# One accumulator in two weight slots, and a new order of decode and eviction in the steps of two chained MLP layers

## The chip, the cores and the metric

The kernel runs on one core of a Trainium2 chip. The metric is device time in microseconds (us) of one execution. Lower is better. Three runs of the kernel before are given, and one execution of it was profiled.

## The reference

A block-wise linear attention with decay gives a token matrix x of 1536 x 512. Two MLP layers follow, each with weights of its own:

```python
h = x @ w_in                                   # 1536x512 @ 512x2048
g = h * np.tanh(log1p(exp(h)))                 # layer 1 (mish)
x = g @ w_out                                  # 1536x2048 @ 2048x512
h = x @ w_in2
g = h * (1.0 / (1.0 + np.exp(-h)))             # layer 2 (silu)
out = g @ w_out2
```

All of it is in 32 bit. The change lies in the two layers; the attention is not touched.

## The kernel before, in words

**Tiling.** The 1536 tokens are three tiles of 512 (t = 0, 1, 2). The hidden size of 2048 is 16 blocks of 128 per layer. Blocks are taken two at a time, so a layer has 8 pairs and the two layers have pairs p = 0 to 15. Pairs 0 to 3 run beside and just behind the attention. From p = 4 on, each pair is one object `Step(p)`, written out by hand as a plan. `NF // 2` is 8, so step 8 is the first of layer 2, step 9 has no plan of its own before and runs the one called `steady`, and step 15 is the last.

**Precision.** Each 32-bit operand is held as a high part `hi` (rounded on ScalarE, `copy`, L237 and others) and a low part `lo` (what is left, a subtraction on GpSimd, L238, or on VectorE). A product is three passes: hi x hi, lo x hi, hi x lo.

**Fewer products.** For token tiles 0 and 1 together a step uses a seven-product scheme on 2 x 2 blocks, for both matrix products: `m1 m5 m6 m2 m7 m3 m4` (input side, L1080 to L1111) and `s1 s5 s6 s2 s7 s3 s4` (output side, L1262 to L1303), six matmuls each. It needs sums of blocks of x (`sums[0]` to `sums[3]`, made once per layer) and sums of blocks of the weights (`sum_pair`, called T for the input side and S for the output side). Step 8 has no T and uses eight plain products instead, `e0` to `e3`. Token tile 2 is computed plainly: `h0`, `h1` (12 matmuls each) and `o0`, `o1` (12 each). A usual step therefore has 42 + 24 + 24 + 42 matmuls of 128 x 512.

**PSUM.** Eight banks `Z[0]` to `Z[7]` are shared by all of it by hand. `quad[0]` is Z0 and Z1, `quad[2]` is Z4 and Z5, `quad[3]` is Z6 and Z7. `o0` and `o1` sum into four banks `po`, which `o1` then adds to the accumulator of tile 2 (L1241; copied on ScalarE, L1239, in step 8). `s1` then copies quad 3 to quad 0 on ScalarE (L1265), and `s6` goes on summing there. `into` (L1273) adds a quad to an accumulator on VectorE (L1279), or in step 8, where the accumulator is new, copies it on ScalarE (L1277).

**Weights.** A block of weights arrives packed, 512 KB, in one of four `slots` (L58, L111). `run_pre` (in plans `p`, `p4`, `p5`) issues two ScalarE activations that begin the decoding (L137, L138); `p4` and `p5` put the intermediate into the free bank Z4 or Z5, and plain `p` leaves it in SBUF. `run_split` (`d`) issues the next small operation of a list: a block takes two VectorE operations (L169, L173), the second of which gives the slot back; the sums of a pair take four on GpSimd (L206). `run_parts` (`w`) takes the next finished weight tile and makes its hi (L237) and lo (L238). After each visit of a plan (between semicolons) `pump` issues the loads for which a slot is free.

**Order.** Each engine runs its instructions in the order in which the plans issue them. A later instruction never passes one that waits.

**Between the layers.** The results of layer 1 stand in three accumulators, `accs[0, t]`. `a0` and `a1` are those of tiles 0 and 1. From them come the block sums of layer 2, partly in place: `s_1` makes the first two, `s_3` writes a0 - a1 into the first half of `a1` (L1338), `s_4` changes the second half of `a0` (L1341), and `s_5` makes the hi parts of sums 3 and 2 on ScalarE; `low3` and `low2` make their lo parts on VectorE (L1309). Tile 0's accumulator of layer 2, `accs[1, 0]`, takes the place of `a0`, and `accs[1, 1]` that of `a1`, so they are first written (L1277) when all that read the old ones has ended. The sums are used in step 9: sum 0 in `m5`, 1 in `m6`, 2 in `m7`, 3 in `m3`.

Of the kernel before, what the change touches and what calls it, by code (L numbers as in the profile page):

```python
# [7 lines left out]
F32 = mybir.dt.float32  # L8
# [9 lines left out]
def decay_attention_mish_silu_kernel(  # L18
# [8 lines left out]
    nc = tc.nc  # L27
    P = 128
# [7 lines left out]
    T = 512  # L36
# [3 lines left out]
    NF = w1.shape[0]  # L40
# [7 lines left out]
    const = ctx.enter_context(tc.tile_pool(name="const", bufs=1))  # L48
    xp = ctx.enter_context(tc.tile_pool(name="xp", bufs=NB))
    accp = ctx.enter_context(tc.tile_pool(name="accp", bufs=1))  # L50
# [4 lines left out]
    ps_o = banks.enter_context(tc.tile_pool(name="ps_o", bufs=2, space=PSUM))  # L55

    ctx.enter_context(tc.manual_schedule())
    slots = [const.tile([P, 1024], F32, name=f"slot{i}") for i in range(4)]  # L58
    arena = const.tile([P, 32, T], F32R, name="arena")
    places = [(arena, k) for k in range(32)]  # L60
    free = list(range(32))
# [5 lines left out]
    def take(weight=False):  # L67
        taken[0] += weight
        k = free.pop(0)
        whole_tile, j = places[k]  # L70
        t = whole_tile[:, j]
        lent[id(t)] = (k, t)
        return t
# [13 lines left out]
    def room():  # L87
        return len(free) > 1 and taken[0] + 2 <= quota[0]
# [13 lines left out]
    held = {}  # L102
# [23 lines left out]
    def split_w(n, i, pair=False):  # L126


        def begin(place=None):
            if place is not None:  # L130
                made[n, i] = place
            decs[n, i] = wdec.tile([P, 512], U32, tag="dec", name="dec")
            uses[n, i] = 1 + pair
            begun[n, i] = tick[0]
            low, high = raws[n, i][:, :, 0], raws[n, i][:, :, 1]
            d = made[n, i] if (n, i) in made else decs[n, i].bitcast(F32)
            nc.scalar.activation(d, high.bitcast(F32), AF.Copy, scale=2.0**-112)  # L137
            nc.scalar.activation(low, low, AF.Copy, scale=TOP3, bias=2.0**-21 - 0.5)  # L138

        def op(k):  # L140
            split_op(k, raws[n, i], decs[n, i], made.get((n, i)))
            if k == 1:
                slots.append(held.pop((n, i)))
                parts.append((decs[n, i].bitcast(F32), (n, i)))

        pre.append(((n, i), begin))
        todo.extend(((n, i), lambda k=k: op(k)) for k in range(2))
# [4 lines left out]
    def run_pre(k=1, age=1, place=None):  # L152
        while k and pre and len(uses) < WD and pre[0][0] in raws and tick[0] - loaded[pre[0][0]] >= age:
            pre.pop(0)[1](place)
            k -= 1

    def used(key):
        if key in uses:
            uses[key] -= 1
            if not uses[key]:  # L160
                del uses[key]

    def split_op(k, raw, d, place):


        low, high = raw[:, :, 0], raw[:, :, 1]
        e = d if place is None else place.bitcast(U32)
        if k == 0:
            nc.vector.scalar_tensor_tensor(  # L169
                out=e, in0=e, scalar=3, in1=low, op0=ALU.logical_shift_left, op1=ALU.bitwise_or  # L170
            )
        else:
            nc.vector.scalar_tensor_tensor(  # L173
                out=d, in0=high, scalar=0x80000000, in1=e, op0=ALU.bitwise_and, op1=ALU.bitwise_or
            )
# [43 lines left out]
    def run_parts(k=None):  # L219
        for _ in range(len(parts) if k is None else min(k, len(parts))):  # L220
            if not room():
                break
            f, key = parts.pop(0)
            homes_of[key] = take(True), take(True)
            hi, lo = [t.rearrange("p (k c) -> p k c", k=2) if len(key) > 2 else t for t in homes_of[key]]
            wtiles[key] = hi, lo
            if len(key) > 2:
                uses_left[key] = 1
            elif key[0] < GF:
                uses_left[key] = (3, 6)[key[1]]  # L230
            elif key[0] < 2 * GF:
                uses_left[key] = (2, 3)[key[1]]
            else:
                uses_left[key] = 2
            ready.add(key)
            used(key)
            nc.scalar.copy(hi, f)  # L237
            nc.gpsimd.tensor_tensor(out=lo, in0=f, in1=hi.bitcast(F32), op=ALU.subtract)  # L238

    def run_split(k, age=1):  # L240
        while k and todo and (todo[0][0] is None or (todo[0][0] == "sum" and not scratch) or begun.get(todo[0][0], 1 << 30) <= tick[0] - age):
            todo.pop(0)[1]()
            k -= 1
# [25 lines left out]
    def warm(n):  # L269
# [12 lines left out]
        out=unit, in_=unit, pattern=[[1, C]], base=1 - C, channel_multiplier=1, compare_op=ALU.not_equal, fill=1.0  # L282
# [260 lines left out]
    accs = {}  # L543
# [117 lines left out]
    def cast(i, f):  # L661
        return lambda: nc.scalar.copy(sums[i][0], f)

    def low(i, f):
        hi, lo = sums[i]
        return lambda: nc.vector.tensor_tensor(out=lo, in0=f, in1=hi.bitcast(F32), op=ALU.subtract)

    def tt(out, in0, in1, op):
        return lambda: nc.vector.tensor_tensor(out=out, in0=in0, in1=in1, op=op)
# [11 lines left out]
    sums = []  # L681
# [136 lines left out]
    for hh in range(2):  # L818
        for p in range(NP):
            h = H - 1 - (2 * p + hh)  # L820
            nc.vector.tensor_tensor_scan(
                out=whole_mask[:, hh, p], data0=lams[:, h : h + 1].to_broadcast([P, C]), data1=unit, initial=0.0,
# [54 lines left out]
    for i, (t, f) in enumerate(steps):  # L877
        n = i + PH
        if n == N:
# [11 lines left out]
                out=eye, in_=eye, pattern=[[1, P]], base=0, channel_multiplier=-1, compare_op=ALU.not_equal, fill=1.0  # L891
# [12 lines left out]
        lows = len(later)  # L904
# [97 lines left out]
    for item in items:  # L1002
# [7 lines left out]
        lows = len(later)  # L1010
# [26 lines left out]
    add, sub = ALU.add, ALU.subtract  # L1037
    tt = nc.vector.tensor_tensor
# [4 lines left out]
    class Step:  # L1043
# [186 lines left out]
        def o1(self):  # L1230
            self.o(1, self.po)
            if self.opens:
                accs[1, 2] = homes[-1].tile([P, 4, T], F32, tag="acc", name="acc")
            if self.seeded:
                return
            acc = accs[self.mm, 2]
            for k in (2, 0, 1, 3):
                if self.opens:
                    nc.scalar.copy(acc[:, k], self.po[k])  # L1239
                else:  # L1240
                    tt(out=acc[:, k], in0=self.po[k], in1=acc[:, k], op=add)  # L1241
# [25 lines left out]
        def s5(self):  # L1267
            self.second(2, 0, 0, True)
            if self.opens:
                accs[1, 0] = accp.tile([P, 4, T], F32, tag="acc", name="acc")  # L1270
            self.into(0, 2, 2, True)

        def into(self, t, a, src, fresh=False):  # L1273
            for k in range(2):
                to = accs[self.mm, t][:, a + k]
                if fresh and self.opens:
                    nc.scalar.copy(to, self.quad[src][k])  # L1277
                else:
                    tt(out=to, in0=self.quad[src][k], in1=to, op=add)  # L1279

# [24 lines left out]
    a0, a1 = accs[0, 0], accs[0, 1]  # L1305
# [8 lines left out]
    lows = {}  # L1314
# [12 lines left out]
    def c(t, k, e):  # L1327
        cast_x(t, k)(e)
# [6 lines left out]
        lows[1] = cast(sums[1], g[1])  # L1335

    def s_3():
        tt(out=a1[:, 0:2], in0=a0[:, 0:2], in1=a1[:, 0:2], op=sub)  # L1338

    def s_4():  # L1340
        tt(out=a0[:, 2:4], in0=a0[:, 2:4], in1=F[:, 0:2], op=sub)  # L1341

    def s_5():
        lows[3] = cast(sums[3], a0[:, 2:4])
        lows[2] = cast(sums[2], a1[:, 0:2])

    def turn(st):
        for i in range(8):
# [9 lines left out]
    def close(st):  # L1358
# [9 lines left out]
        for k, c in PIECES:  # L1368
            tt(out=acc[:, k, c], in0=st.po[k][:, c], in1=acc[:, k, c], op=add)
            nc.sync.dma_start(out_tiles(2)[:, k, c], acc[:, k, c])  # L1370

    extras = {"x2": x2, "s_1": s_1, "s_3": s_3, "s_4": s_4, "s_5": s_5}
    extras |= {f"low{i}": lambda i=i: low(i) for i in range(4)}
    extras |= {f"c{t}{k}": lambda t=t, k=k: c(t, k, nc.gpsimd if k > t else nc.vector) for t in range(2) for k in range(2)}
    extras |= {"p": lambda: run_pre(1, 0), **{f"p{i}": lambda i=i: run_pre(1, 0, st.Z[i]) for i in (4, 5)}, "d": lambda: run_split(1, 0), "w": lambda: run_parts(1)}
    tail = "m7 d d; m3; m4 ts; h0 a0 q0 n4 w; l0 p4 h1 a1 q1 w; l1 p5 o0 d d d d; o1 w w d d; s1 d d; s5 w; s6; s2 w; s7; s3; s4 p4"
    steady = "m1 p5 d d d d; m5; m6 w w; m2 d d; " + tail
    plans = {
        GF: "m1 p4 p5; m5; m6 d d d d; m2 w w d d; " + tail,
        NF // 2 - 1: "m1 p5 d d d d; m5; m6 w w; m2; m7; m3 ts; m4 n4 q0; h0 a0 l0; h1 a1 l1 q1; "  # L1380
        "s1; s5 table w; s6 p w; s2; s7 c01 seed; s3 c00; s4 c11 c10; o0 s_1; o1",
        NF // 2: "e0 low0 low1 x2 d d; e1 s_4 p w; e2 s_3 d d; e3; h0 a0 w l0 d d d d ts; h1 a1 s_5 l1 n4 q0 w q1 w low3; p o0; o1; s1 p; s5 d d w d d w; s6 low2 d d d d; s2; s7 w w; s3; s4 p4",
        NF - 1: "m1 p5 d d d d; m5; m6 w w d d d d; m2; m7 w w; m3 ts; m4 n4 q0; h0 a0 l0; h1 a1 l1 q1; s1; s5; s6; s2; s7; s3; s4; o0; o1",
    }
    adder[0] = nc.gpsimd
# [5 lines left out]
    for p in range(GF, NF):  # L1391
        st = Step(p)
# [55 lines left out]
```

## Time and profile before

| what | value |
|---|---|
| median of 3 runs | 556.21 us (556.08 to 556.86) |
| profiled execution, its own time | 556.43 us |
| its span, first to last instruction | 554.3 us |
| TensorE (PE) busy | 542.9 us, 98% |
| VectorE (DVE) busy | 401.9 us, 72% |
| ScalarE (ACT) busy | 340.8 us, 61% |
| GpSimd (POOL) busy | 287.8 us, 52% |
| granted TensorE clock | 0.998 |

A busy share is time in which an engine had an instruction running. PE is TensorE's matmul, PEld its weight load, which runs ahead of the matmuls. SPq is the queue that issues the loads of weights. In a timeline, the bracket at the end of a row is the engine's idle time just ahead of the row and the instruction that ended it.

### The profile page before, as it was taken

Reading aid. Unit: us, or ns where it says so; the run is one execution under the profiler, and the core shown is the slowest. Engines: PE = TensorE matmul, PEld = TensorE weight load, DVE = VectorE, ACT = ScalarE, POOL = GpSimd, SP = SyncE. Lnnn points to the kernel's source line nnn. Section 1 sums busy time; section 2 is a strip of 40 time slices with the busy share of each in tenths; the row PEclk is TensorE's granted clock in tenths of the full one; section 3 lists DMA queues with packets and bytes.
Section 4 is the critical chain, followed back from the end, with each engine's and each line's share of the span. In section 5 each row is a group of like instructions: output and inputs, shape, how many; then the busy total and the mean of one; then the engine's idle time right before and its main releaser. Section 6 shows DMA issues by size and latency. Waiting matters only on the chain.

```text
span 554.3 us, 8859 instructions
## 1 busy us (share of the span) xinstructions
PE 542.9 (98%) x3306; PEld 437.5 (79%) x3306; DVE 401.9 (72%) x639; ACT 340.8 (61%) x622; POOL 287.8 (52%) x269
## 2 busy tenths in 40 slices
PE   9999999999999999999999989999999999999995
PEld 6888778888877788888878767888887888888875
DVE  4887956994575695877867976686768595867684
ACT  4778553862654847566665877666575747565631
POOL 3555620322033775939220574957666675849610
PEclk9999999999999999999999999999999999999999
DMA  8993450231112222222200222222212122220006
GB/s 297 406 315 125 141 167 1 79 113 38 39 43 70 77 76 78 76 77 76 77 0 2 76 76 77 76 77 74 78 40 78 37 77 76 77 76 1 1 0 228
DMA packets 14602, 49.85 MB, mean 90 GB/s; under 512 B 1632, under 2 KB 1888, under 8 KB 14560
## 3 DMA queue, kind: packets, MB, share of 16 engines
q1 hardware_dynamic: 14560, 49.29, 26.3%
q8 instruction: 26, 0.43, 0.3%
q14 instruction: 16, 0.13, 0.1%
HBM read 46.14 MB, written 3.15 MB: 89 GB/s over the span
## 4 chain that ended last, share of the span: by engine, by line
PE 82%; DVE 9%; ACT 5%; issue 2%; POOL 1%; DMA 0%; SPq 0%; DVEq 0%; POOLq 0%; ACTq 0%
PE z L1255 19%; PE z L1066 16%; PE z L1157 10%; PE z L1212 9%; PE ph L588 7%; PE po L616 6%; PE pu L637 5%; PE b L733 1%; PE s L353 1%; PE px L406 1%; DVE xl L1309 1%; PE a L733 1%; PE warm L273 1%; DVE dec L173 1%; PE px L396 1%
## 5 line engine op out<-in xcount | busy, mean ns | idle before, releaser
L238 POOL TENSOR_TENSOR arena<-dec,arena 128x512 fp32r<-128x512 f32 x49 | 64.3, 1319 | 118.9 <-ACT arena L237 113.2
L1255 PE MATMUL z<-arena 128*128 128x512 f32 x376 | 97.7, 394 | 2.1 <-ACT acc L1277 1.2
L1279 DVE TENSOR_TENSOR acc<-z,acc 128x512 f32<-128x512 f32 x136 | 84.6, 683 | 10.8 <-PE z L1255 10.8
L1255 PEld LDWEIGHTS z<-arena 128*128 128x128 f32 x376 | 69.6, 188 | 20.2 <-ACT z L1265 3.1
L1149 POOL TENSOR_TENSOR arena<-F,arena 128x1024 fp32r<-128x1024 f32 x20 | 48.2, 2412 | 49.3 <-ACT arena L1148 49.3
L1157 PE MATMUL z<-xh,arena 128*128 128x512 f32 x168 | 53.8, 389 | 0.0
L238 POOL TENSOR_TENSOR arena<-t,arena 128x512 fp32r<-128x512 f32 x34 | 45.8, 1354 | 15.4 <-ACT arena L237 15.4
L237 ACT CAST arena<-dec 128x512 fp32r<-128x512 f32 x56 | 34.7, 620 | 29.7 <-DVE dec L173 29.6
L1212 PE MATMUL z<-arena 128*128 128x512 f32 x188 | 52.4, 390 | 0.3 <-DVE F L1139 0.3
L1066 PE MATMUL z<-xh,arena 128*128 128x512 f32 x182 | 50.0, 390 | 0.3 <-DVE z L1098 0.2
L138 ACT ACTIVATE slot<-slot 128x512 uint32<-128x512 uint32 x64 | 42.7, 668 | 0.0
L1212 PEld LDWEIGHTS z<-arena 128*128 128x128 f32 x188 | 35.2, 188 | 8.1 <-DVE F L1139 0.8
L237 ACT CAST arena<-t 128x512 fp32r<-128x512 f32 x38 | 23.5, 619 | 28.7 <-POOL t L206 23.0
L1066 PEld LDWEIGHTS z<-xh,arena 128*128 128x128 f32 x182 | 34.0, 188 | 8.3 <-DVE z L1098 0.7
L588 PE MATMUL ph<-xh,arena 128*128 128x512 f32 x124 | 39.2, 393 | 0.0
L137 ACT ACTIVATE z<-slot 128x512 f32<-128x512 f32 x40 | 25.4, 636 | 19.0 <-DVE acc L1279 19.0
L1157 PEld LDWEIGHTS z<-xh,arena 128*128 128x128 f32 x168 | 31.5, 188 | 6.5
L169 DVE SCALAR_TENSOR_TENSOR z<-z,slot 128x512 uint32<-128x512 uint32 x40 | 27.8, 695 | 10.3 <-ACT slot L138 10.0
L1157 PE MATMUL z<-xl,arena 128*128 128x512 f32 x88 | 34.2, 389 | 0.0
L637 PE MATMUL pu<-arena 128*128 128x512 f32 x132 | 33.8, 400 | 0.2 <-ACT arena L237 0.2
L206 POOL TENSOR_TENSOR t<-dec 128x256 f32<-128x256 f32 x42 | 31.3, 745 | 0.0
L616 PE MATMUL po<-arena 128*128 128x512 f32 x128 | 30.7, 393 | 0.1
(250 smaller groups left out, 1228.3 us busy)
## 6 DMA issues: line engine op xcount, KB each, us to landing
slot<-w SPq DMA_DIRECT2D x64, 512.0 KB, 4.2
xslot<-x SPq DMA_DIRECT2D x24, 512.0 KB, 7.5
out<-F SPq DMA_DIRECT2D x8, 256.0 KB, 2.1
out<-acc SPq DMA_DIRECT2D x3, 256.0 KB, 2.7
out<-acc SPq DMA_DIRECT2D x2, 128.0 KB, 2.5
factors<-lam SPq DMA_DIRECT2D x1, 0.0 KB
```

The lines of the kernel that those rows point to most:

```text
L138: nc.scalar.activation(low, low, AF.Copy, scale=TOP3, bias=2.0**-21 - 0.5)
L237: nc.scalar.copy(hi, f)
L238: nc.gpsimd.tensor_tensor(out=lo, in0=f, in1=hi.bitcast(F32), op=ALU.subtract)
L588: nc.tensor.matmul(ph, lhsT=wi[wsel][:, kk * P : (kk + 1) * P], rhs=xt[xsel][:, kk, :], start=(i == 0), stop=(i == 3 * KD - 1),)
L616: nc.tensor.matmul(po[t][j][:, c], lhsT=lhsT, rhs=rhs, start=(first and wsel + gsel == 0), stop=(last and gsel == 1 and c.stop == T),)
L637: nc.tensor.matmul(banks[j], lhsT=wtiles[f, 1][ws][:, js[j] * P : js[j] * P + P], rhs=gts[f, t][gs], start=(i < 2), stop=(i >= len(passes) ...
L1066: nc.tensor.matmul(self.Z[dst], lhsT=w[ws][:, kk * P : (kk + 1) * P], rhs=x[xx][:, kk, :], start=(start and i == 0), stop=True, skip_group ...
L1149: low.tensor_tensor(out=lo, in0=f, in1=hi.bitcast(F32), op=sub)
L1157: nc.tensor.matmul(z, lhsT=w[ws][:, kk * P : (kk + 1) * P], rhs=x[xx][:, kk, :], start=(i == 0), stop=True, skip_group_check=True,)
L1212: nc.tensor.matmul(banks[k], lhsT=lhsT, rhs=rhs, start=(j == 0 and ws + gs == 0 and not self.seeded), stop=True, skip_group_check=True,)
L1255: nc.tensor.matmul(self.quad[dst][k], lhsT=w[ws][:, k * P : (k + 1) * P], rhs=g[gs], start=(start and i == 0), stop=True, skip_group_check ...
L1279: tt(out=to, in0=self.quad[src][k], in1=to, op=add)
```

## The change

- `accs[1, 0]` gets storage of its own: slots 2 and 3 become the two halves of one tile, `slab`. When the two output-side weight blocks of step 8 are decoded, their slots go to a list `kept` that is never used again, and `s5` of step 8 takes `slab` as the accumulator. From then on there are two slots instead of four.
- `s_3` writes a0 - a1 into the first half of `a0`. `s_5` is split into `hi2` and `hi3`, which move from `h1` to `s7` of step 8; `low2` moves from `s6` to `s3`, and `low3` from `h1` of step 8 to `m6` of step 9, behind that visit's VectorE addition.
- In step 8 the decoding of the next blocks starts earlier (`p` in `h1` instead of with `o0`), and the two copies of `s4` go to VectorE (`into` with t = 1 and a = 2).
- `steady`: two of the four `d` of `m1` move behind `m6`'s product and addition.
- `tail` (steps 4 to 6 and 9 to 14): the two decodes start as `p6` (bank Z6) behind `l0` and `p4` behind `q1`, instead of `p4` behind `l0` and `p5` behind `l1`; the first `d` stands ahead of `l1`.
- `o1` adds its banks in the order 0, 1, 2, 3 instead of 2, 0, 1, 3, other than in step 8.

```diff
@@ slots
-    slots = [const.tile([P, 1024], F32, name=f"slot{i}") for i in range(4)]
+    slab = const.tile([P, 2048], F32, name="slab")
+    slots = [const.tile([P, 1024], F32, name=f"slot{i}") for i in range(2)]
+    slots += [slab[:, 1024 * i : 1024 * i + 1024] for i in range(2)]
+    kept = []
@@ split_w, op
-                slots.append(held.pop((n, i)))
+                (kept if n // 2 == NF // 2 and i else slots).append(held.pop((n, i)))
@@ o1
-            for k in (2, 0, 1, 3):
+            for k in (2, 0, 1, 3) if self.opens else range(4):
@@ s5, into
-                accs[1, 0] = accp.tile([P, 4, T], F32, tag="acc", name="acc")
+                accs[1, 0] = slab.rearrange("p (a c) -> p a c", a=4)
...
-                    nc.scalar.copy(to, self.quad[src][k])
+                    (nc.vector.tensor_copy if t and a else nc.scalar.copy)(to, self.quad[src][k])
@@ block sums of layer 2
-        tt(out=a1[:, 0:2], in0=a0[:, 0:2], in1=a1[:, 0:2], op=sub)
+        tt(out=a0[:, 0:2], in0=a0[:, 0:2], in1=a1[:, 0:2], op=sub)
...
-    def s_5():
-        lows[3] = cast(sums[3], a0[:, 2:4])
-        lows[2] = cast(sums[2], a1[:, 0:2])
+    def hi(i):
+        lows[i] = cast(sums[i], a0[:, 2 * i - 4 : 2 * i - 2])
@@ plans
-for i in (4, 5)}
+for i in (4, 5, 6, 7)}
-    tail = "m7 d d; m3; m4 ts; h0 a0 q0 n4 w; l0 p4 h1 a1 q1 w; l1 p5 o0 d d d d; o1 w w d d; s1 d d; s5 w; s6; s2 w; s7; s3; s4 p4"
-    steady = "m1 p5 d d d d; m5; m6 w w; m2 d d; " + tail
+    tail = "m7 d d; m3; m4 ts; h0 a0 q0 n4 w; l0 p6 h1 a1 q1 p4 w; d l1 d o0 d d; o1 w w d d; s1 d d; s5 w; s6; s2 w; s7; s3; s4 p4"
+    steady = "m1 p5 d d; m5; m6 d d w w; m2 d d; " + tail
-        NF // 2: "e0 low0 low1 x2 d d; e1 s_4 p w; e2 s_3 d d; e3; h0 a0 w l0 d d d d ts; h1 a1 s_5 l1 n4 q0 w q1 w low3; p o0; o1; s1 p; s5 d d w d d w; s6 low2 d d d d; s2; s7 w w; s3; s4 p4",
+        NF // 2: "e0 low0 low1 x2 d d; e1 s_4 p w; e2 s_3 d d; e3; h0 a0 w l0 d d d d ts; h1 a1 p l1 n4 q0 w q1 w d d; o0; o1 ; s1 p w; s5 d d; s6 d d d d w; s2; s7 hi2 w hi3 w; s3 low2; s4 p4",
+        NF // 2 + 1: steady.replace("m6", "m6 low3"),
```

## Rows read from the trace of the kernel before

**Rows 1.** The page, busy time of each engine, share of the span, instructions.

```profile
PE 542.9 (98%) x3306; PEld 437.5 (79%) x3306; DVE 401.9 (72%) x639; ACT 340.8 (61%) x622; POOL 287.8 (52%) x269
```

**Rows 2.** The chain that ended last, step 11: start, length, what.

```profile
393.24 9.69 PE z L1066 x42
...
408.37 5.44 PE z L1212 x24
413.81 9.67 PE z L1255 x42
```

**Rows 3.** Windows, step 8 and step 9's input side: length, busy time of engines.

```profile
295.59:330.53 34.94, 32.53 (x139) 25.60 (x138) 32.41 (x37) 27.60 (x48) 15.33 (x13) 1.00 0.19 61
330.53:342.30 11.77, 10.41 (x43) 7.65 (x42) 5.34 (x9) 8.79 (x17) 8.77 (x10) 1.00 0.28 90
```

**Rows 4.** Timeline of step 8, ScalarE, VectorE and TensorE: start, length, engine, line.

```profile
313.50 1.03 ACT L1308 CAST xh<-acc 128x1024 fp32r<-128x1024 f32 x1
...
316.04 0.68 DVE L1191 TENSOR_TENSOR F<-z,F 128x512 f32<-128x512 f32 x1
...
317.99 0.39 PE L1255 MATMUL z<-arena 128*128 128x512 f32 x1
...
318.32 0.66 ACT L137 ACTIVATE dec<-slot 128x512 f32<-128x512 f32 x1
...
319.44 2.03 ACT L1239 COPY acc<-z 128x512 f32<-128x512 f32 x4
...
320.06 1.67 PE L1255 MATMUL z<-arena 128*128 128x512 f32 x6 [0.54 <-ACT acc L1239]
...
322.01 3.03 PE L1255 MATMUL z<-arena 128*128 128x512 f32 x12 [0.28 <-ACT z L1265]
...
323.47 1.07 ACT L1277 COPY acc<-z 128x512 f32<-128x512 f32 x2
...
325.65 2.04 ACT L1277 COPY acc<-z 128x512 f32<-128x512 f32 x4
...
326.28 4.42 PE L1255 MATMUL z<-arena 128*128 128x512 f32 x18 [1.24 <-ACT acc L1277]
```

**Rows 5.** Timeline of step 9's input side, TensorE.

```profile
334.82 0.73 PE L1066 MATMUL z<-sh,more 128*128 128x512 f32 x2 [0.78 <-ACT z L1082]
...
338.08 1.19 PE L1066 MATMUL z<-sh,arena 128*128 128x512 f32 x4 [0.25 <-DVE z L1090]
```

**Rows 6.** Timeline of step 8, VectorE and GpSimd, both working on SBUF.

```profile
316.64 3.56 DVE L1149 TENSOR_TENSOR arena<-F,arena 128x1024 fp32r<-128x1024 f32 x2
...
317.03 4.33 POOL L238 TENSOR_TENSOR arena<-t,arena 128x512 fp32r<-128x512 f32 x2 [0.15 <-ACT arena L237]
...
320.12 2.31 DVE L1309 TENSOR_TENSOR xl<-acc,xh 128x1024 fp32r<-128x1024 f32 x1
```

**Rows 7.** Timeline of step 11, all engines, a steady step.

```profile
397.80 0.69 DVE L1090 TENSOR_TENSOR z<-z,F 128x512 f32<-128x512 f32 x1
...
398.55 0.30 PEld L1066 LDWEIGHTS z<-sh,more 128*128 128x128 f32 x2 [0.29 <-DVE z L1090]
...
400.25 0.70 DVE L1098 TENSOR_TENSOR z<-z,F 128x512 f32<-128x512 f32 x1 [1.75 <-PE z L1066]
...
411.21 0.61 ACT L237 CAST arena<-t 128x512 fp32r<-128x512 f32 x1
...
411.73 0.63 ACT L137 ACTIVATE z<-slot 128x512 f32<-128x512 f32 x1
...
414.39 2.48 DVE L1241 TENSOR_TENSOR acc<-z,acc 128x512 f32<-128x512 f32 x4
...
415.77 1.17 ACT L1265 COPY z<-z 128x512 f32<-128x512 f32 x2 [0.63 <-DVE acc L1241]
416.39 1.23 PEld L1255 LDWEIGHTS z<-arena 128*128 128x128 f32 x6 [0.28 <-ACT z L1265]
```

**Rows 8.** Instructions of the weight loads, L111, from 262 to 425 us.

```profile
DMA to landing us min/median/max: 3.5/4.2/4.7
```

More of the change, by code (lines that the diff above doesn't have):

```diff
@@ L1370, in close @@
             nc.sync.dma_start(out_tiles(2)[:, k, c], acc[:, k, c])
-    extras = {"x2": x2, "s_1": s_1, "s_3": s_3, "s_4": s_4, "s_5": s_5}
+    extras = {"x2": x2, "s_1": s_1, "s_3": s_3, "s_4": s_4, "hi2": lambda: hi(2), "hi3": lambda: hi(3)}
     extras |= {f"low{i}": lambda i=i: low(i) for i in range(4)}
     extras |= {f"c{t}{k}": lambda t=t, k=k: c(t, k, nc.gpsimd if k > t else nc.vector) for t in range(2) for k in range(2)}
-    extras |= {"p": lambda: run_pre(1, 0), **{f"p{i}": lambda i=i: run_pre(1, 0, st.Z[i]) for i in (4, 5)}, "d": lambda: run_split(1, 0), "w": lambda: run_parts(1)}
-    tail = "m7 d d; m3; m4 ts; h0 a0 q0 n4 w; l0 p4 h1 a1 q1 w; l1 p5 o0 d d d d; o1 w w d d; s1 d d; s5 w; s6; s2 w; s7; s3; s4 p4"
-    steady = "m1 p5 d d d d; m5; m6 w w; m2 d d; " + tail
+    extras |= {"p": lambda: run_pre(1, 0), **{f"p{i}": lambda i=i: run_pre(1, 0, st.Z[i]) for i in (4, 5, 6, 7)}, "d": lambda: run_split(1, 0), "w": lambda: run_parts(1)}
+    tail = "m7 d d; m3; m4 ts; h0 a0 q0 n4 w; l0 p6 h1 a1 q1 p4 w; d l1 d o0 d d; o1 w w d d; s1 d d; s5 w; s6; s2 w; s7; s3; s4 p4"
+    steady = "m1 p5 d d; m5; m6 d d w w; m2 d d; " + tail
     plans = {
```

## Prediction

> **What bounds the kernel now.** I read the page's busy times first: PE is busy for 542.9 of 554.3 us [rows 1], so the change cannot shorten the work; it can only close holes in PE's stream, and what the other engines do matters only where PE waits for it. The chain of waits comes second, because it shows what a step costs without holes: 24 matmuls of the plain products take 5.44 us [rows 2], 0.2267 us each, so the 42 of an input or output side should take 9.52. They take 9.69 and 9.67 [rows 2]: each side of a steady step hides a hole of 0.17 or 0.15 us that is too short to show as idle PE. The windows come third, since they show where the large holes are. Step 8 has 138 matmuls (48 + 24 + 24 + 42), 31.28 us, and takes 34.94; step 9's input side should take 9.52 and takes 11.77 [rows 3]. So 3.66 + 2.25 = 5.9 us are lost at the change of layers. The timeline comes last and names who is late there.
>
> **Steady steps.** Input side: `m7` writes Z6 again, and may not before L1090 (`m6`'s addition) has read it. VectorE runs L1090 behind all four decode operations, and PE's weight load waits 0.29 us for it [rows 7]. With two of them moved behind L1090, it can start when `m6`'s product ends, 393.24 + 18 x 0.2267 = 397.3, instead of at 397.80, and end about 398.0; `m7` is due at 393.24 + 24 x 0.2267 = 398.7. The hole closes: 0.17 us. What the two decodes delay: ScalarE's casts of the second block, and behind them `m2`'s activations, some 1.3 us; they have their cover in the 1.75 us that VectorE idles ahead of L1098 [rows 7], and the decodes end about 0.65 us before L1098 is due. That is the margin; without it `m4` waits for L1098.
> Output side: `s6` waits 0.28 us for L1265, and L1265 waits 0.63 us for L1241, the second of `o1`'s four additions [rows 7]. In the new order bank 0 comes first, 0.62 us (2.48 / 4) earlier. And the second decode starts where the cast at 411.21 stood and no longer behind it at 411.73 [rows 7], so the VectorE operations ahead of L1241 end 0.5 us earlier. Together 1.1 us against a wait of 0.28: closed, 0.15 us. Z6 as a decode bank is free (its last reader is `n4`) and is read before `s1` writes it; Z4 is read before `s5` does.
> The new `tail` serves nine steps (4 to 6, 9 to 14), the new `steady` seven beside step 9 (5, 6, 10 to 14): 9 x 0.15 + 7 x 0.17 = **2.5 us**. Bounds: 0, if another wait takes over in each; 2.5, as nothing more is lost there.
>
> **Two slots.** A slot is free at its block's L173, and its next block's decode starts some 11.5 to 12 us later in a steady step (half a step of 9.69 + 5.44 + 5.44 + 9.67 = 30.24, less the decode itself); in step 8 and 9 about 7. The load lands in 3.5 to 4.7 us [rows 8]. SPq carries nothing else in this stretch. Cost: nothing, covered by at least 2 us. The `slab` halves are free when `s5` needs them: the blocks in them were decoded in `e0` and `e2`.
>
> **Step 8.** PE loses 0.70 at `s5` (317.99 + 6 x 0.2267 = 319.35, starts 320.06), 0.59 at `s6` and 1.55 at `s7` [rows 4], and the rest at `o0`, which the change leaves.
> ScalarE decides all three. Before, the casts of `s_5` (two of 1.03) run at 313.50; the cast of `q1` has to wait for L1191 in any case, which ends at 316.72 [rows 4]. Now `p` (1.12, from 318.32 to 319.44 [rows 4]) runs in that place, so the copies L1239 begin at 318.3 instead of 319.44. The first ends at 318.8: `s5` waits no more. L1265 begins at 320.2 and its first copy ends at 320.8: `s6` is 0.1 late instead of 0.59.
> Then the second `p` runs to 322.35, and a cast `w` that needs L173. Its two VectorE operations stand behind L1149 and a GpSimd subtraction that ends at 317.03 + 4.33 = 321.36 [rows 6]; they end at 322.7. Cast to 323.3, two copies of `s5` to 324.3 (1.07 [rows 4]), the first copy of `s6` to 324.85. `s7` starts at 324.9, was 326.28 [rows 4]: gain 1.4, between 0.9 (the cast waits once more) and 1.8 (not at all). With 18 matmuls behind it step 9 starts at 329.0, was 330.53: **1.5 us**.
>
> **Step 9's input side.** It lost 2.25: among it 0.78 for L1082, queued on ScalarE behind copies and a decode, and 0.25 for L1090 [rows 5]. ScalarE now does, from 325.4, three casts `w` (0.5), the copies of `s7`, `hi2` and `hi3` (1.0 each) and the decode `p4` (1.12), to 331.0; L1082 ends at 331.6, `m6` is due at 329.0 + 12 x 0.2267 = 331.7. Covered, by 0.1. VectorE is the new risk: behind `s3`'s additions (end 329.0) come `low2` (1.2), the two copies that left ScalarE (1.3), two decodes (1.4), L1090 (0.7), `low3` (1.2), two decodes, L1098.
> What `low2` and `low3` cost is read from rows 6: two L1149 take 3.56 and two L238 4.33 when they meet, and L1309 takes 2.31. Where a VectorE operation and a GpSimd one both work on SBUF, they take turns: L1309, issued at 320.12, has 1.2 us left when L238 ends at 321.36. So each may cost 1.2 alone, or 2.4. GpSimd subtracts T's two low parts just beside `low2`, and a weight's beside `low3`. With no collision L1090 ends at 333.9 and L1098 at 337.2, and `m7` (due 334.4) and `m4` (due 337.2) lose 0.1 together. With one, at `low2`, L1090 ends at 334.75 and L1098 at 338.05: 0.35 + 0.55 = 0.9. With two, 2.15. I take one, since the two engines reach `low2` and T's first subtraction within 0.1 us of each other and only one can be first. Gain 2.25 - 0.9 = **1.35**, less 0.3, because the activations behind come late and `o0` waits for `l0`.
> The Trainium skill (SBUF — State Buffer, "SBUF: two separate sides") says that a VectorE operation with two SBUF inputs and a GpSimd operation that reads SBUF lock each other out for a whole instruction, first come, first served. Rows 6 agree. By it `low2` and `low3` can both lose, which is the first rival; a reading as shared bandwidth would make both only somewhat slower, near the likeliest sum.
>
> **Sum.** 2.5 + 1.5 + 1.35 - 0.3 = 5.05. The profiled execution took 556.43, so 551.4; the median of the runs shown lies 0.2 lower, so 551.2, and I say **551.3 us**.
>
> **Rivals.**
> Both lows collide: step 9 then gains 0.1 (2.25 - 2.15), the sum is 2.5 + 1.5 + 0.1 = 4.1, **552.2**. For it: GpSimd has work at both places. Against: an order of arrival must fall the same way twice.
> No collision: 2.5 + 1.5 + 2.15 = 6.15, **550.1**. For it: GpSimd's sums of T now start before the second block's subtraction, and may be through.
> The steady gains are taken by another wait: in the input side L1098 behind the late decodes (margin 0.65), in the output side `s6` still behind L1265. Then only 2.55 of the change of layers stays, **553.8**. For it: the gain is two holes of 0.15, and ScalarE's order changes in every step.
> Slower: two slots starve. Each load waits for L173; if landing took over 11.5 us, each decode would start late, VectorE and ScalarE would wait in order behind it, and PE at the next product of that weight. To lose the 5.05 and 1.1 more, steps 9 to 14 must lose 1.0 each, landing 12.5 us or more: **557.3**. Against: 4.7 at most, and the same bytes.
> No change: the waits of step 8 move on within ScalarE and return at step 9 as L1082 (margin 0.1) and L1098, and the steady holes stay: **556**.
>
> **Chances.** Forecast 0.42, both collide 0.18, none 0.15, steady gains lost 0.13, no change 0.06, slower 0.06. 0.2% is 1.1 us, about what a measurement of this kernel can tell from no change; all of the first four are beyond it: faster 0.88, same 0.06, slower 0.06. The range reaches from 549.5 (no collision and the 1.8 at `s7`) to 554.0 (steady gains lost, with 0.2 for the bound at `s7`); outside it lie no change, slower, and little more.
>
> **What would show it.** In the profile after: steady sides of 9.52 us in the chain of waits, no PE wait on L1090 or L1265 outside steps 7, 8 and 15; no wait on L1239; `s7` of step 8 some 3.5 + 1.4 us after `s5`'s start; step 9 about 1.5 us earlier; `low2` or `low3` at 2.3 us. Wrong it would be if L111 loads gated L137, if PE waited for L1098 in steady steps, or if step 8's copies still held `s5`.

## The result and the profile after

Five runs of the changed kernel have a median of 551.02 us (550.84 to 551.51), five of the kernel before 556.30 us (556.08 to 556.86). The ratio is 0.9904, with an interval of 0.9889 to 0.9918: faster by 0.96%, some 5.3 us. The forecast was 551.3, in a range of 549.5 to 554.0. The profiled execution took 551.02 us, its span is 549.1, and the granted clock was 0.999. The first line of the page, which answers to [rows 1]:

```profile
PE 539.3 (98%) x3306; PEld 438.7 (80%) x3306; DVE 404.0 (74%) x641; ACT 338.2 (62%) x620; POOL 288.3 (53%) x269
```

The number of matmuls is the same, and PE is still busy for 98% of the span. That PE's busy time fell by 3.6 us with the same work is part of the story: a hole shorter than a matmul does not show as idle PE.

The diff adds three lines, so L1066 of before is now L1069, L1090 is L1093, L1098 is L1101, L1241 is L1244, L1255 is L1258, L1265 is L1268, L1277 is L1280, and L1309 is L1312. The chain of waits, a steady step (start, length, what), answers to [rows 2]:

```profile
389.30 9.52 PE z L1069 x42
398.82 5.44 PE z L1160 x24
404.26 5.44 PE z L1215 x24
409.70 9.52 PE z L1258 x42
```

Both sides have come down to 42 x 0.2267 = 9.52 us. In VectorE's timeline of that step, beside [rows 7], the first addition has moved ahead of the second block's decode, and the second addition keeps 0.56 us of idle time ahead of it (1.75 before):

```profile
393.49 0.70 DVE L1093 TENSOR_TENSOR z<-z,F 128x512 f32<-128x512 f32 x1 [1.20 <-ACT arena L240]
...
396.14 0.70 DVE L1101 TENSOR_TENSOR z<-z,F 128x512 f32<-128x512 f32 x1 [0.56 <-PE z L1069]
```

L1093 is put down to a cast here, but it also needs `m6`'s product, which is due at 389.30 + 18 x 0.2267 = 393.38; it starts 0.11 later. The windows of step 8 and of step 9's input side (length, then busy time of PE, PEld, DVE, ACT, POOL with counts, clock, DMA share, GB/s), for [rows 3]:

```profile
294.86:327.93 33.07, 32.11 (x139) 25.67 (x138) 30.52 (x36) 27.79 (x49) 15.75 (x14) 1.00 0.09 32
327.93:338.82 10.89, 10.11 (x44) 7.73 (x42) 8.35 (x11) 6.64 (x14) 6.47 (x6) 1.00 0.24 76
```

Step 8 lost 3.66 us before and now loses 33.07 - 31.28 = 1.79; step 9's input side lost 2.25 and now loses 10.89 - 9.52 = 1.37. The timeline of step 8's end, for [rows 4]:

```profile
312.41 0.66 ACT L140 ACTIVATE dec<-slot 128x512 f32<-128x512 f32 x1
...
316.91 0.39 PE L1258 MATMUL z<-arena 128*128 128x512 f32 x1
...
317.14 2.04 ACT L1242 COPY acc<-z 128x512 f32<-128x512 f32 x4
...
319.05 1.77 DVE L172 SCALAR_TENSOR_TENSOR dec<-dec,slot 128x512 uint32<-128x512 uint32 x1
319.05 1.10 ACT L1268 COPY z<-z 128x512 f32<-128x512 f32 x2
319.72 2.62 PEld L1258 LDWEIGHTS z<-arena 128*128 128x128 f32 x12 [0.35 <-ACT z L1268]
...
321.58 0.62 ACT L240 CAST more<-dec 128x512 fp32r<-128x512 f32 x1 [0.28 <-DVE dec L176]
...
322.11 2.04 ACT L1280 COPY slab<-z 128x512 f32<-128x512 f32 x4
...
323.71 4.38 PE L1258 MATMUL z<-arena 128*128 128x512 f32 x18 [0.96 <-ACT slab L1280]
```

`s1` starts at 316.91, and `s7`, 24 matmuls later, is due at 322.35; it starts at 323.71, so 1.36 are lost on the way, most of it at `s7` itself (the row shows 0.96 of it as idle PE). Before, the same 24 matmuls took 326.28 - 317.99 = 8.29, a loss of 2.85 [rows 4]. `s5` waits no more, since the four copies of tile 2 (L1242) no longer queue behind the first `p`, which has moved to 312.41. What holds `s7` is the queue ahead of its copy on ScalarE, and in it the cast at 321.58, which idled 0.28 us for VectorE: the decode L172 took 1.77 us.

Step 9's input side, for [rows 5] and [rows 6]:

```profile
326.88 1.30 POOL L241 TENSOR_TENSOR more<-dec,arena 128x512 fp32r<-128x512 f32 x1
...
327.45 1.82 DVE L1312 TENSOR_TENSOR sl<-acc,sh 128x1024 fp32r<-128x1024 f32 x1
...
328.14 2.28 POOL L241 TENSOR_TENSOR arena<-t,more 128x512 fp32r<-128x512 f32 x1
...
330.47 0.73 PE L1069 MATMUL z<-sh,arena 128*128 128x512 f32 x2 [0.56 <-POOL arena L241]
...
332.88 1.29 POOL L241 TENSOR_TENSOR arena<-dec,arena 128x512 fp32r<-128x512 f32 x1 [1.20 <-ACT arena L240]
333.14 0.70 DVE L1093 TENSOR_TENSOR z<-z,F 128x512 f32<-128x512 f32 x1 [1.27 <-PE z L1069]
...
333.74 1.51 DVE L1312 TENSOR_TENSOR xl<-acc,xh 128x1024 fp32r<-128x1024 f32 x1
...
335.18 0.69 DVE L172 SCALAR_TENSOR_TENSOR z<-z,slot 128x512 uint32<-128x512 uint32 x1
...
336.57 0.69 DVE L1101 TENSOR_TENSOR z<-z,F 128x512 f32<-128x512 f32 x1
...
337.32 1.19 PE L1069 MATMUL z<-xh,arena 128*128 128x512 f32 x4 [0.22 <-DVE z L1101]
```

PE stops twice. In `m5` it waits for a low part of T: two matmuls before it was due at 327.93 + 8 x 0.2267 = 329.74 and came at 330.47, 0.73 late. The other 0.64 of the 1.37 lie behind that row, most of it at `m4`, which waits for L1101. The waits on L1082 and L1090 of before are gone.

**Where the time came from.** From step 4's first matmul to the end of the span the kernel before took 380.89 us (554.3 - 173.41), the one after 375.74 (549.1 - 173.36), 5.15 less; ahead of step 4 the code is the same but for the slots.

| part | before | after | gain | forecast |
|---|---|---|---|---|
| 9 steady output sides | 9.65 to 9.68 each | 9.52 each | 1.3 | 1.35 |
| 7 steady input sides | 9.67 to 9.69 each | 9.52 each | 1.2 | 1.2 |
| step 8 | 34.94 | 33.07 | 1.87 | 1.5 |
| step 9, input side | 11.77 | 10.89 | 0.88 | 1.35 - 0.3 |
| sum | | | 5.2 | 5.05 |

### The profile page after: what moved, and what is told of

Same layout as the page of the kernel before. It is cut to its first block, busy times and chain, and to the rows that moved or that the text cites. A ratio compares the mean times of both kernels' runs of the same rounds, so it can differ in the third digit from the quotient of the medians.

```text
span 549.1 us, 8856 instructions
## 1 busy us (share of the span) xinstructions
PE 539.3 (98%) x3306; PEld 438.7 (80%) x3306; DVE 404.0 (74%) x641; ACT 338.2 (62%) x620; POOL 288.3 (53%) x269
## 4 chain that ended last, share of the span: by engine, by line
PE 79%; DVE 9%; ACT 5%; DMA 4%; issue 1%; SPq 1%; POOL 0%; DVEq 0%
PE z L1258 19%; PE z L1069 17%; PE z L1160 11%; PE z L1215 9%; PE ph L591 7%; PE po L619 6%; PE pu L640 5%; DMA xslot<-x 2%; DMA slab<-w 2%; PE b L736 1%; PE a L736 1%; DVE xl L1312 1%; DVE dec L176 1%; DVE arena L1152 1%; DVE dec L172 1%
## 5 line engine op out<-in xcount | busy, mean ns | idle before, releaser
L1258 PE MATMUL z<-arena 128*128 128x512 f32 x376 | 96.0, 390 | 1.0 <-ACT slab L1280 1.0
L1258 PEld LDWEIGHTS z<-arena 128*128 128x128 f32 x376 | 70.3, 188 | 16.6 <-ACT slab L1280 1.4
L1215 PE MATMUL z<-arena 128*128 128x512 f32 x188 | 52.4, 390 | 0.0
L1282 DVE TENSOR_TENSOR acc<-z,acc 128x512 f32<-128x512 f32 x76 | 47.7, 681 | 4.8 <-PE z L1258 4.8
L1069 PE MATMUL z<-xh,arena 128*128 128x512 f32 x182 | 50.1, 391 | 0.6 <-DVE z L1101 0.5
L1282 DVE TENSOR_TENSOR slab<-z,slab 128x512 f32<-128x512 f32 x60 | 38.6, 683 | 10.3 <-PE z L1258 10.2
L1069 PEld LDWEIGHTS z<-xh,arena 128*128 128x128 f32 x182 | 33.9, 188 | 8.7 <-DVE z L1101 1.3
L172 DVE SCALAR_TENSOR_TENSOR z<-z,slot 128x512 uint32<-128x512 uint32 x34 | 23.5, 692 | 16.4 <-ACT slot L141 16.2
L140 ACT ACTIVATE z<-slot 128x512 f32<-128x512 f32 x34 | 21.7, 638 | 17.9 <-DVE slab L1282 11.9
```

Source lines behind the costliest of these rows:

```text
L1069: nc.tensor.matmul(self.Z[dst], lhsT=w[ws][:, kk * P : (kk + 1) * P], rhs=x[xx][:, kk, :], start=(start and i == 0), stop=True, skip_group ...
L1215: nc.tensor.matmul(banks[k], lhsT=lhsT, rhs=rhs, start=(j == 0 and ws + gs == 0 and not self.seeded), stop=True, skip_group_check=True,)
L1258: nc.tensor.matmul(self.quad[dst][k], lhsT=w[ws][:, k * P : (k + 1) * P], rhs=g[gs], start=(start and i == 0), stop=True, skip_group_check ...
```

## The experiments

The theory is the prediction's: four separate gains (two holes in the steady steps, ScalarE's queue in step 8, the sums in step 9), with VectorE and GpSimd taking turns as the loss that stays. Its rivals were that one part does the work of all, that two slots cost something, and that the loss at step 9 comes from the queue on VectorE and not from turn-taking.

**e1_bank_order**: before, with the new order of banks alone.

```diff
-            for k in (2, 0, 1, 3):
+            for k in (2, 0, 1, 3) if self.opens else range(4):
```

> The kernel before with one line of the change, the order 0, 1, 2, 3 of the additions of o1. Theory: bank 0 is added one operation (0.62 us) earlier, the copy L1265 ends before s6 is due, and each of nine output sides falls from 9.67 to 9.52: 1.35 us less in all, input sides at 9.69 as before. Rival: the additions stand behind the decodes, so the order alone leaves part of the wait, and output sides stay above 9.6.

Measured: 555.27 us, ratio 0.9977 (0.9968 to 0.9986). The chain of waits, one input and one output side:

```profile
392.66 9.70 PE z L1066 x42
...
413.24 9.52 PE z L1255 x42
```

All nine steady output sides came to 9.52, the input sides stayed at 9.65 to 9.70. From step 4 to the end the kernel took 1.39 us less. The order of four additions closes the output hole alone.

**e2_decode_tail**: before, with the new `tail` alone.

```diff
-... l0 p4 h1 a1 q1 w; l1 p5 o0 d d d d; ...
+... l0 p6 h1 a1 q1 p4 w; d l1 d o0 d d; ...
```

> The kernel before with the new tail alone (banks Z6 and Z4, first decode operation ahead of l1). Theory: the additions of o1 begin 0.5 us earlier, which is more than the 0.28 that s6 waits, so this alone closes the output sides too: 9.52, 1.35 us less, and nothing is to be had from both together. Rival: half a microsecond is eaten up by the copy's own queue, and the sides stay above 9.6.

Measured: 554.68 us, ratio 0.997 (0.9958 to 0.9981). The same view:

```profile
392.73 9.68 PE z L1066 x42
...
413.29 9.52 PE z L1255 x42
```

The output sides came to 9.52 here too, and the stretch from step 4 on is 1.18 us shorter. So the two edits of the output side close one and the same hole, and each suffices: in the change, one of them is worth nothing.

**e3_input_side**: before, with the new `steady` alone.

```diff
-    steady = "m1 p5 d d d d; m5; m6 w w; m2 d d; " + tail
+    steady = "m1 p5 d d; m5; m6 d d w w; m2 d d; " + tail
```

> The kernel before with the new steady alone (two decode operations behind the addition L1090 in m6). Theory: seven input sides fall from 9.69 to 9.52, 1.2 us, and step 9's own, which uses this plan as well, loses its wait for L1090, 0.3 to 0.4 more: 1.5 us less in all, output sides at 9.67. Rival: the late decodes hold up L1098, and m4 waits in its place, sides at 9.6 or more.

Measured: 553.99 us, ratio 0.9956 (0.9942 to 0.9971). All steady input sides came to 9.52, and the output sides stayed at 9.61 to 9.71. Step 9's input side took 11.25 instead of 11.77, and PE's wait of 0.78 for L1082 stood there unchanged; the wait for L1090 was gone. From step 4 on it took 2.07 us less, more than the 1.2 + 0.5 of these parts. The rest is a hole of step 8 at `o0`, which was 0.32 us smaller in this run; it is taken up below.

**e4_layers_only**: after, with the old order of banks, `tail` and `steady`, so that only the storage and the change of layers stay.

```diff
-            for k in (2, 0, 1, 3) if self.opens else range(4):
+            for k in (2, 0, 1, 3):
...
-    steady = "m1 p5 d d; m5; m6 d d w w; m2 d d; " + tail
+    steady = "m1 p5 d d d d; m5; m6 w w; m2 d d; " + tail
```

> The changed kernel with the old tail, the old steady and the old order of o1: the accumulator in two slots, the later block sums and step 8's new plan alone, with two slots from step 9 on. Theory: step 8 takes 33.1 as in the changed kernel, step 9's input side 10.9 to 11.5, since the four decodes stand ahead of L1090 again, and the steady sides take 9.69 and 9.67: 2.2 to 2.8 us less than before. Rival: two slots can be had only with the new order, so loads come late and the steps from 10 to 14 take more than 30.24.

Measured: 553.42 us, ratio 0.9945 (0.993 to 0.996). The steady sides have their holes again (9.60 to 9.72), so two slots go with the old order too. The windows of step 8 and of step 9's input side, and VectorE's second low part and addition in step 9:

```profile
295.82:329.24 33.42, 32.10 (x140) 25.67 (x138) 30.52 (x36) 27.84 (x49) 15.72 (x14) 1.00 0.10 32
329.24:339.62 10.38, 9.81 (x44) 7.80 (x42) 9.08 (x13) 7.83 (x15) 9.09 (x8) 1.00 0.32 103
```

```profile
335.09 1.48 DVE L1312 TENSOR_TENSOR xl<-acc,xh 128x1024 fp32r<-128x1024 f32 x1
...
337.10 0.70 DVE L1101 TENSOR_TENSOR z<-z,F 128x512 f32<-128x512 f32 x1 [0.53 <-PE z L1069]
```

Step 8 is 34.94 - 33.42 = 1.52 us shorter, the forecast's 1.5. Step 9 surprised: 10.38, better than the whole change's 10.89. With all four decodes ahead of the first addition, only `low3` stands between the two additions, and the second idles 0.53 us instead of being late. So in step 9 the new `steady`, which gains 0.17 us in each of the seven other steps, costs 0.5. It does so only with `low3` in that place: in e3, without it, the same edit gained step 9 0.52 us.

**e5_low3_m5**: after, with `low3` one visit earlier.

```diff
-        NF // 2 + 1: steady.replace("m6", "m6 low3"),
+        NF // 2 + 1: steady.replace("m5", "m5 low3"),
```

> The changed kernel with low3 one visit earlier, in m5 of step 9, where VectorE idles 1.27 us. Theory: m4 waits for L1101 (0.22 us shown, 0.6 lost) because low3 and two decodes stand ahead of it; with low3 out of that row L1101 starts when m7 ends, and step 9's input side falls from 10.89 to about 10.3. Rival: the wait comes from the decodes alone, and moving low3 only delays L1093 by as much, so the side stays at 10.8 to 11.

Measured: 550.55 us, ratio 0.9897 (0.9882 to 0.9911). Step 9's input side took 10.36. VectorE's timeline:

```profile
331.76 1.22 DVE L1312 TENSOR_TENSOR xl<-acc,xh 128x1024 fp32r<-128x1024 f32 x1
...
335.76 0.70 DVE L1101 TENSOR_TENSOR z<-z,F 128x512 f32<-128x512 f32 x1 [0.56 <-PE z L1069]
```

`low3` fits into the time in which VectorE waited for `m6` (1.27 us in after), meets no GpSimd operation, takes 1.22 instead of 1.51, and the wait on L1101 is gone. The wait of 0.55 us in `m5` is unchanged. So the two stops of step 9 are two things: the second is VectorE's queue between the additions.

**e6_t_first**: after, with T's parts made in another order (`r` moves the first waiting weight tile to the end of the list), so that GpSimd reaches T's low part sooner.

```diff
-... s6 d d d d w; s2; s7 hi2 w hi3 w; s3 low2; s4 p4"
+... s6 d d d d r; s2; s7 hi2 w hi3 w; s3 low2 w; s4 p4"
```

> The changed kernel with the low part of T's first half made ahead of that of the second weight block (which is needed only by m3). Theory: m5 waits 0.56 us (0.73 lost) because GpSimd's subtraction of T stands behind another one and then waits for low2; put first it ends before m5 needs it, and step 9's input side falls from 10.89 to about 10.2. Rival: low2 then waits for GpSimd in place, the operations behind it come late, and m4 loses what m5 gains.

Measured: 550.47 us, ratio 0.9899 (0.9884 to 0.9914); step 9's input side 10.58. The timeline of its second half:

```profile
332.30 1.28 POOL L241 TENSOR_TENSOR arena<-dec,arena 128x512 fp32r<-128x512 f32 x1 [0.91 <-ACT arena L240]
332.60 2.06 DVE L1312 TENSOR_TENSOR xl<-acc,xh 128x1024 fp32r<-128x1024 f32 x1
...
336.73 0.73 PE L1069 MATMUL z<-xh,more 128*128 128x512 f32 x2 [0.76 <-DVE z L1101]
```

The wait in `m5` is gone, so it was T's low part that came late. But PE arrives sooner at `m6`, VectorE's `low3` now meets GpSimd's subtraction (332.30 to 333.58) and takes 2.06 instead of 1.51, and the wait for L1101 grew from 0.22 to 0.76. Of the 0.73 us gained, 0.4 went back.

**e7_loads_twice**: after, with each weight load of pairs 9 to 15 issued twice into the same slot, so that a load takes about twice as long.

```diff
-        nc.sync.dma_start(held[n, i]..., wsrc[...])
+        for _ in range(2 if n >= NF + 2 else 1):
+            nc.sync.dma_start(held[n, i]..., wsrc[...])
```

> The changed kernel with each load of the pairs 9 to 15 done twice, one behind the other, so that a slot's data are there some 4 us later; the result is the same data. Theory: a slot has 11.5 us or more in steady steps and the loads keep within it, so the sides stay at 9.52 and the time within 0.3 us of the changed kernel's. Rival: two slots are close to starving, the decodes start late and steps 9 to 14 take more than 29.92 each.

Measured: 555.24 us, ratio 0.9976 (0.9967 to 0.9986), 4.7 us slower than `e5_low3_m5`, which shared its chip and whose step 9 is 0.5 us shorter than that of after. All steady sides from step 9's output on stayed at 9.52: there, even twice the load hides behind two slots, as the theory had it. It missed step 9, whose input side took 16.50 us (the profiled execution took 556.21, about 1 us more than the median). Its timeline (line numbers one higher), windows of it, and two rows of the chain of waits:

```profile
334.68 0.62 ACT L141 ACTIVATE z<-slot 128x512 f32<-128x512 f32 x1 [4.56 <-DMA slot<-w]
...
336.37 0.70 DVE L1094 TENSOR_TENSOR z<-z,F 128x512 f32<-128x512 f32 x1 [5.00 <-ACT F L1090]
...
337.13 2.08 PE L1070 MATMUL z<-sh,arena 128*128 128x512 f32 x4 [3.24 <-DVE z L1094]
```

```profile
330.00:333.00 3.00, 3.00 (x13) 2.50 (x14) 1.26 (x2) 0.12 (x1) 1.17 (x1) 1.00 0.49 154
...
337.00:340.00 3.00, 2.87 (x7) 2.29 (x8) 2.91 (x3) 0.00 (x0) 1.22 (x1) 0.50 0.54 175
340.00:342.50 2.50, 2.50 (x8) 1.92 (x7) 1.43 (x3) 1.77 (x4) 1.07 (x1) 0.50 0.20 75
```

```profile
325.13 5.06 DMA slot<-w
330.21 4.39 DMA slot<-w
```

The second block's decode idled 4.56 us for its load; the copy and the addition of `m6` stand behind it, and PE stopped for 3.24. The edit did more here than double one load. A slot's second load waits for its first, and the other slot's loads stand behind both on SPq (28 times it waited for a load into a slot to land before it issued one of weights, in after never), so the second block's data were there at 330.21 + 4.39 = 334.60, 12.2 us after its slot came free (322.39). So the rival "two slots starve" is a real mechanism with its place at the change of layers, where two blocks are wanted soon after their slots come free, and not in the steady steps. In after itself it does not bite: the weight loads of this stretch landed like this, for [rows 8]:

```profile
DMA to landing us min/median/max: 3.5/3.7/5.0
```

**e8_scalar_copies**: after, with `s4`'s two copies of step 8 on ScalarE again.

```diff
-                    (nc.vector.tensor_copy if t and a else nc.scalar.copy)(to, self.quad[src][k])
+                    nc.scalar.copy(to, self.quad[src][k])
```

> The changed kernel with the two copies of s4 in step 8 on ScalarE again. Theory by the trace of the changed kernel: L1085 then ends about 1 us later, at 331.2 at the latest, and m6 is not due before 331.5, so nothing changes. Rival, by the sum of the prediction, where L1085 had a margin of 0.1: m6 waits about 0.9 us, the time rises by as much.

Measured: 551.95 us, ratio 0.9921 (0.9906 to 0.9936); step 9's input side took 11.35, 0.46 more than after. The timeline:

```profile
333.64 1.29 POOL L241 TENSOR_TENSOR arena<-dec,arena 128x512 fp32r<-128x512 f32 x1 [1.70 <-ACT arena L240]
334.02 1.99 DVE L1312 TENSOR_TENSOR xl<-acc,xh 128x1024 fp32r<-128x1024 f32 x1
...
338.07 1.20 PE L1069 MATMUL z<-xh,arena 128*128 128x512 f32 x4 [0.69 <-DVE z L1101]
```

The cost is neither nothing nor a wait of `m6`. ScalarE runs the decode behind the copies, so the cast of the first block and GpSimd's subtraction behind it come late: 333.64 - 328.21 = 5.43 us into step 9, against 332.88 - 327.93 = 4.95 in after. `low3` starts 5.81 us into the step in both kernels. In after the subtraction has 0.43 us left by then, here 0.91, so `low3` takes 1.99 instead of 1.51, and the wait for L1101 grows from 0.22 to 0.69. The copies on VectorE are worth 0.46 us, by way of a meeting that they shorten.

**e9_step8_order**: after, with step 8 reordered by what the runs above showed: the second `p` and the casts earlier, `low2` behind `s4`, T's part first as in e6, and the copy of tile 2's fourth bank behind L1268's two.

```diff
-... h1 a1 p l1 n4 q0 w q1 w d d; o0; o1 ; s1 p w; s5 d d; s6 d d d d w; s2; s7 hi2 w hi3 w; s3 low2; s4 p4"
+... h1 a1 p l1 n4 q0 p w q1 w d d; o0; o1; s1; s5 d d; s6 d d d d; s2 w; s7 hi2 r w hi3 w; s3; s4 low2 w p4"
@@ o1
-            for k in (2, 0, 1, 3) if self.opens else range(4):
+            for k in (2, 0, 1) if self.opens else range(4):
@@ s1, behind the copies of quad 3
+            if self.opens:
+                nc.scalar.copy(accs[1, 2][:, 3], self.po[3])
```

> The changed kernel with step 8 put in another order: the second p between q0 and its cast instead of behind s1, the copy of po's last bank behind L1268, the sums of T ahead of the weight's low part, T's low parts ahead of the second weight block's, low2 behind the two copies of s4. Theory: s7 waits 0.96 us (1.27 lost) only because a decode and a cast stand on ScalarE ahead of the copies L1280; without them it waits for nothing and step 8 takes 31.8 to 32.1 instead of 33.07; step 9's input side loses 0.6 to 1.0 instead of 1.37. 1.2 to 2.0 us less than the changed kernel. Rival: the work only moves, o1's copies and s5 come late in its place, and step 8 stays at 33.

Measured: 549.36 us (548.41 to 550.37), ratio 0.9878 (0.9859 to 0.9897). The windows of step 8 and of step 9's input side:

```profile
294.52:326.29 31.77, 31.77 (x139) 25.67 (x138) 30.16 (x36) 27.33 (x48) 13.18 (x13) 1.00 0.10 33
326.29:336.37 10.08, 10.02 (x43) 7.73 (x42) 8.46 (x11) 6.90 (x14) 9.11 (x7) 1.00 0.27 81
```

PE shows no idle time in step 8, which is 0.49 above its 31.28 us, and `s7` waits no more. Step 9's input side loses 0.56. Both are a little better than expected, and the whole is 1.7 us below `after_again`. So what was left at `s7` was a matter of order: with the second `p` ahead of the copies of tile 2, the wait is gone without another engine taking the work. The edits were made together; which of them would have been enough is not shown.

**e10_steps_4_7_8**: e9, with the new order of `steady` in the plan of step 7, and in that of step 4 the start of the second decode one visit later.

```diff
-        GF: "m1 p4 p5; m5; m6 d d d d; ...
-        NF // 2 - 1: "m1 p5 d d d d; m5; m6 w w; ...
+        GF: "m1 p4; m5 p5; m6 d d d d; ...
+        NF // 2 - 1: "m1 p5 d d; m5; m6 d d w w; ...
```

> As the run before, and the input sides of the two steps that kept their old plans: step 7 gets the new order of steady (0.17 us by the theory), and step 4 its second decode start one visit later, behind the copy L1089 that m6's addition needs (its side takes 10.66 against 9.52; 0.5 to 0.9 us less by the theory). Together 0.7 to 1.0 us less than the run before. Rival: the second decode then holds up L1101 in step 4 and only a part of it, under 0.3, is gained.

Measured: 548.23 us (547.92 to 548.67), ratio 0.9852 (0.9837 to 0.9867). It beats both kernels. The view of PE's waits by releaser lists only these (us in total, times, longest us):

```profile
PE warm L276 <- DVE zeros L264: 1.0, 1, 1.0
PE ph L591 <- ACT arena L240: 0.2, 1, 0.2
```

Step 4's input side took 10.14 instead of 10.66, step 7's 9.52 instead of 9.69: 0.69 together, and the rival's "under 0.3" did not come. None of the waits lies in steps 4 to 15. Holes too short to show as idle PE are left: the input sides of steps 4 and 9 (10.14 and 10.16) are still some 0.6 us above 9.52.

**after_again**: the changed kernel once more, on the chip of e9 and e10.

> The changed kernel once more, on the same chip as the two runs beside it: 550.8 to 551.5 us, sides of 9.52.

Measured: 551.07 us (550.6 to 551.11), ratio 0.9901 (0.9886 to 0.9915), with sides of 9.52, step 8 at 33.07 and step 9's input side at 10.85. So e10 is 2.8 us faster than the change on the same chip.

## Why the prediction was right, point by point

**The bound.** That only holes in PE's stream count held in every run: e8 took work from VectorE and lost, and the change made VectorE and GpSimd busier (404.0 and 288.3 us) and won.

**Steady steps, 2.5 us.** Right in size and place: all sixteen sides came to 9.52. Two things in the working need mending. The output side was argued as "together 1.1 us against a wait of 0.28", as if both edits were wanted; e1 and e2 show that either closes the hole. And the margin ahead of the second addition was put at 0.65 us and is 0.56. That rival was near: 0.56 us is less than one of the decodes (0.69) that were moved there.

**Two slots, nothing.** Right; loads landed in 3.5 to 5.0 us. The cover was given as over 11.5 us in steady steps and 7 in steps 8 and 9. e7 agrees with the difference: loads issued twice hid in the one and cost a stop of 3.24 us in step 9, where the second block's data came 12.2 us after its slot was free. The rival was priced in the wrong place (1.0 us in each of steps 9 to 14).

**Step 8, 1.5 us.** Right for what was argued: from `s1` to `s7` the loss fell from 2.85 to 1.36, by 1.49, and e4 shows 1.52 for the step with the steady edits undone. `s5` waits no more, `s6` is about 0.2 late where 0.1 was said, and `s7` still waits for the cast behind L172, as forecast; e9 removes that wait by order alone. Of the remaining 0.38 us of after's 1.87, 0.35 lie at `o0`, which lost 0.64 before and 0.29 after. VectorE works from the second operation of `s_1` to the one that `o0` waits for without a pause. That second operation starts straight behind the first in some runs (298.85 in after), and 0.46 us later, with no releaser shown but the operation ahead of it, in others (before, e1 and e4). Before:

```profile
299.94 1.23 DVE L1334 TENSOR_TENSOR F<-F,acc 128x1024 f32<-128x1024 f32 x1 [0.46 <-DVE F L1332]
```

It follows no edit in particular (e2 and e3, with the old step 8, have it sooner). Its cause stays open, and it was not forecast. That it covers the 0.17 by which step 9 fell short (0.88 against 1.05) is luck.

**Step 9, 1.35 - 0.3.** The sum was close (0.88), the way was not. The failed step is "With one, at `low2`, L1090 ends at 334.75 and L1098 at 338.05: 0.35 + 0.55 = 0.9". One meeting at `low2` there was, but the step charged it all to VectorE's queue. VectorE waited for GpSimd's subtraction to end at 326.88 + 1.30 = 328.18 and needed 1.1 more (327.45 + 1.82 = 329.27); GpSimd, issued at 328.14, then stood until 329.27 and took 2.28 us, not 1.3. That second turn fell on T's low part, which `m5` wants, and no line of the prediction had PE waiting for GpSimd there: 0.73 us. The trace of before already had this wait, which the prediction's account of step 9 left out:

```profile
332.84 0.73 PE L1066 MATMUL z<-sh,arena 128*128 128x512 f32 x2 [0.33 <-POOL arena L238]
```

L1093 was not late at all (1.27 idle, for PE). The loss behind it, 0.64 against 0.55, came from `low3` and two decodes standing between two additions; e4 and e5, which keep the meeting at `low2` and have no idle PE but the 0.55 in `m5`, show that it does not hang on it. And `low3` did meet GpSimd too: the subtraction of 332.88 ended at 334.17, and `low3`, issued at 333.74, took 1.51 where it takes 1.22 alone in e5. So both lows collided, which was the first rival, but VectorE lost 0.60 and 0.29 by it, and not the 1.2 that the prediction charged for each. A meeting cost a little less than what was left of the other operation: `low3` lost 0.29 with 0.43 left here, 0.84 with 0.98 left in e6, 0.77 with 0.91 left in e8. The 0.3 set aside for late activations at `o0` was not lost: the 48 plain matmuls behind step 9's input side took 2 x 5.44 us. So a loss of 0.9 + 0.3 was forecast and 1.37 measured, close in size and by another way.

The Trainium skill (SBUF — State Buffer, "SBUF: two separate sides") has the two engines lock each other out, a whole instruction at a time. This case's rows agree: of the operations issued at 327.45 and 328.14, each ends 1.1 to 1.2 us after the end of the one ahead of it, about its length alone (1.2 and 1.3).

## What to carry to other kernels

On an engine that is busy for 98% of the span, count the work of a stretch, multiply by the pace of a stretch without holes, and compare: here 0.15 us per side showed in no busy share, and 16 sides made half the gain. When two edits aim at one wait, try each alone: either was enough. When a change moves a plan that is also used in a special step (step 9 ran `steady` with one more operation in it), work that step out anew: the same edit gained 0.17 us in seven steps and cost 0.5 in the eighth.

## What the runs showed of the hardware that was not expected

In e7 PE's granted clock was 1.00 from 330 to 333 us, fell while PE stood for 3.24 us, and was 0.50 from 337 to 342.5, which is 1.2 of 2.4 GHz: pairs of matmuls took 1.05 us instead of 0.62. From 337.13 on, the 12 matmuls of `m7` and `m3` took 5.29 us, up to 342.42; at 0.2267 they would take 2.72. So 2.57 of the 6.98 us that step 9's input side lost came on top of the wait. The stops of up to 1.24 us [rows 3, 4] left the mean clock of their windows at 1.00. A long wait can cost more than its length.

Turn-taking between VectorE and GpSimd was forecast for subtractions. It also holds for the decode's bit operation: the L172 at 319.05 in after, with both inputs in SBUF, was issued while the second of two GpSimd subtractions ran until 320.27 and took 1.77 us; the later one of the same step takes 0.69. The two subtractions:

```profile
315.77 4.50 POOL L241 TENSOR_TENSOR arena<-t,arena 128x512 fp32r<-128x512 f32 x2
```
